# Softmax on ScalarE while weights are narrowed: the added constant and the normalization change engines

## The chip, the cores and the metric

The kernel runs on 1 core of one Trainium2 chip. The metric is the device time of one execution in microseconds (us); less is better. Engines: PE is TensorE, DVE is VectorE, ACT is ScalarE, POOL is GpSimd, SP issues DMAs.

## The reference

Three layers follow each other: a local attention, a feed-forward layer and eight experts with a balanced gate. What the change touches is the softmax of the first.

```python
scores = scale * np.matmul(q, k.transpose(0, 1, 3, 2)) + bias   # 2 batches, 8 heads, 768 tokens, 64 wide
scores = np.where(keep, scores, -1000000000.0)                  # 8 global keys, 96 local ones
a = np.exp(scores - np.max(scores, axis=-1, keepdims=True))
a = a / (np.sum(a, axis=-1, keepdims=True) + 1e-09)
attn = np.matmul(a, v)                                          # then (1536, 512)
h = x @ w_in; x = (h * (1.0 / (1.0 + np.exp(-h)))) @ w_out      # w_in (512, 2048), w_out (2048, 512)
```

Then each of 8 experts adds `P[:, e] * (max(x @ w1[e], 0) @ w2[e])`, with `P` from eight rounds of row and column normalization. `w_in` and `w_out` arrive as 64-bit floats.

## The kernel before

**Attention.** Twelve query tiles of 128 tokens, `k` = 0 to 11; each is worked in two units (`k`, `m`) of four heads. `att_turn` transposes q and k, `att_scores` does the softmax of one unit, `att_flip` transposes the weights, `att_out` multiplies by v and writes the tile `x1` as a rounded part `xh` (ACT, line 813) and a remainder `xl` (DVE, line 814). In `att_scores`, for each of two pairs of heads: PE writes the scores; DVE adds the distance table and takes the minimum (line 755); ACT takes the exponential and its sum (line 759); DVE adds 1e-9 to two sums (line 763) and inverts them (line 764); POOL multiplies each head's row by its inverse (line 767). A unit with `k` = 0 or 6 works on 128 keys, all others on 256.

**Narrowing.** Each of 16 slices of `w_in` and `w_out` is loaded as 64-bit words (`ra`, `rb`, at most 3 slices at a time, lines 129 and 132) and made a 32-bit float `wf` in `narrow`: ACT takes an absolute value `m` (line 197), DVE does four bit operations for each half (lines 203, 205, 207, 209), 8 in a slice, 128 in all. `split` rounds a slice to a high part on ACT (line 224) and takes the low part on POOL (line 225). A narrowed slice is stored to memory by a DMA on ACT's queue (line 179) for later blocks, and only then is its `wf` buffer free; there are five.

**Feed-forward layer.** Hidden steps: PE multiplies (lines 241 to 243), ACT takes a tanh (line 260), DVE makes `g` (line 261), ACT rounds it to `hh` (line 262), POOL or DVE takes the remainder `hl` (line 264), and two steps later PE multiplies by `w_out` (line 280). Steps 0 to 7 take half of the first 512 tokens each, with slices 0 to 3; from step 8 on a step takes all 512 and one slice.

**Order.** `banded` first runs tiles 0 and 1 (`startup` is true), then tiles 2 and 3 beside steps 0 to 7, then tiles 4 to 7 beside the rest of the first token block (`narrowing` is true for both), then the rest. In `go`, attention, narrowing (`pump`) and splitting (`feed`) are written between the steps at a set rate. A scheduler then places the instructions of each engine from that program; each engine works its queue in order. The constants' pool has a pad of `PAD_L` bytes that keeps the later addresses.

`copy` already chooses an engine by the same condition:

```python
        if self.startup or self.narrowing:
            self.nc.scalar.activation(dst, src, AF.Copy)
        else:
            self.nc.vector.tensor_copy(dst, src)
```

Of the kernel before, what the change touches and what calls it, by code (L numbers as in the profile page):

```python
# [8 lines left out]
F32 = mybir.dt.float32  # L9
# [5 lines left out]
AF = mybir.ActivationFunctionType  # L15
ALU = mybir.AluOpType
# [4 lines left out]
P = 128  # L21
# [7 lines left out]
EPS = 1e-9  # L29
# [7 lines left out]
RING = 4  # L37
HB = TB // 2
ORDER = 0, 5, 4, 3, 6, 1, 2
PAD_L, PAD_R = 224, 96  # L40
HALF, LINE = 64, 256
TINY = 1.125 * 2.0**-15

# [5 lines left out]
class Kernel:  # L49
# [29 lines left out]
    def setup(self, const, pre):  # L79
        nc = self.nc  # L80
        n16 = const.tile([P, 2, 4], U16, tag="n16", name="n16")
        for i, src in enumerate((self.n_global, self.n_local)):
            nc.sync.dma_start(
                n16[:, i, :], src.bitcast(U16).rearrange("(o f) -> o f", o=1).broadcast_to([P, 4])
            )
        self.att_load(0, pre)
        self.att_load(1, const)
        self.ident = const.tile([P, P], F32, tag="ident", name="ident")
        make_identity(nc, self.ident)
        rel, key = self.places(pre)  # L90
        self.ones = const.tile([P, P], F32, tag="ones", name="ones")
        nc.gpsimd.memset(self.ones, 1.0)

        ps = self.aps("warm")
        for _ in range(WARM):
            nc.tensor.matmul(ps[:, :P], self.ident, self.ident, start=True, stop=True)

        half = const.tile([P, 2, 4], F32, tag="half", name="half")
        nc.vector.tensor_copy(half, n16)
        nf = const.tile([P, 2], F32, tag="nf", name="nf")  # L100
        nc.vector.tensor_copy(nf, n16[:, :, 3].bitcast(I16))
        for i in (2, 1, 0):
            nc.vector.scalar_tensor_tensor(nf, nf, 65536.0, half[:, :, i], op0=ALU.mult, op1=ALU.add)
        self.ng, self.nl = nf[:, 0:1], nf[:, 1:2]
        fl = const.tile([P, 3], F32, tag="fl", name="fl")
        nc.vector.tensor_scalar(fl[:, 0:1], self.nl, 1.0, None, op0=ALU.is_ge)
        nc.vector.scalar_tensor_tensor(fl[:, 1:2], self.nl, float(L + 1), fl[:, 0:1], op0=ALU.is_le, op1=ALU.mult)
        flag = const.tile([P, 1], I32, tag="flag", name="flag")
        nc.vector.scalar_tensor_tensor(flag, self.ng, float(G), fl[:, 1:2], op0=ALU.is_le, op1=ALU.mult)
        self.flag = flag  # L110

        const.tile([P, PAD_L // 4], F32, tag="pad", name="pad")
        for _ in self.att_turn(0, const):
            pass
        self.tables(const, pre, rel, key)
# [613 lines left out]
    def att_scores(self, k, m):  # L729


        nc, pool = self.nc, self.ap
        a = self.att[k]
        qT, kT = a["qT"], a["kT"]
        n = W if k % self.QT else P
        a["s", m] = s = pool.tile([P, 4, W], F32, tag="s", name=f"s_{k}_{m}", bufs=LAG + 1)
        st = pool.tile([P, 3, 4], F32, tag="st", name=f"st_{k}_{m}", bufs=LAG + 2)
        banks = [self.aps(f"s_{k}_{m}_{j}") for j in range(2)]
        dst = [bank[:, x * W:x * W + n] for x in range(2) for bank in banks]
        ops = ((0, 0), (0, 1), (1, 0))[:3 if len(qT) > 1 else 1]  # L740
        for x in range(2):
            c = 2 * m + x
            for i, (y, z) in enumerate(ops):
                for j in range(2):
                    jj = slice(j * self.D, (j + 1) * self.D)
                    nc.tensor.matmul(
                        dst[2 * x + j], qT[y][jj, c * P:(c + 1) * P], kT[z][jj, c, W - n:],
                        start=i == 0, stop=i == len(ops) - 1,
                    )
        for x in range(2):  # L750
            for h in (2 * x, 2 * x + 1):
                th = self.tab[4 * m + h]
                sx = s[:, h, W - n:]

                nc.vector.tensor_tensor_reduce(  # L755
                    out=sx, in0=dst[h], in1=th[:, :W] if n == W else th[:, W:], scale=1.0, scalar=BIGMIN,
                    op0=ALU.add, op1=ALU.min, accum_out=st[:, 0, h:h + 1],
                )
                nc.scalar.activation(
                    sx, sx, AF.Exp, bias=st[:, 0, h:h + 1], scale=-1.0, accum_out=st[:, 1, h:h + 1]  # L760
                )
            two = slice(2 * x, 2 * x + 2)
            nc.vector.tensor_scalar(st[:, 2, two], st[:, 1, two], EPS, None, op0=ALU.add)  # L763
            nc.vector.reciprocal(st[:, 2, two], st[:, 2, two])  # L764
            for h in (2 * x, 2 * x + 1):
                sx = s[:, h, W - n:]
                nc.gpsimd.tensor_scalar(sx, sx, st[:, 2, h:h + 1], 1.0, op0=ALU.mult, op1=ALU.mult)  # L767
            yield

    def att_flip(self, k, m):  # L770
# [425 lines left out]
```

## Time and profile before

| what | value |
|---|---|
| median of 3 runs | 1407.94 us (1407.59 to 1408.5) |
| the profiled execution | 1407.18 us, its span 1405.3 us |
| PE busy in the span | 1375.1 us (98%), 8552 matmuls |
| DVE busy | 728.6 us (52%) |
| ACT busy | 487.8 us (35%) |
| POOL busy | 555.0 us (39%) |

The span runs from the first to the last instruction. The shares are means over parts of the program with different limits, so the first 160 us, which hold the change, are to be read by themselves.

### The profile page before, as it was taken

The numbers are of one execution on the slowest core, as the hardware profiler recorded it, in microseconds if no ns is written. First come the engines' busy times: TensorE is split into PE (matmuls) and PEld (weight loads), VectorE is DVE, ScalarE is ACT, GpSimd is POOL, SyncE is SP. The second block draws the span as 40 slices with busy tenths as digits, with TensorE's granted clock in tenths as the row PEclk, the third lists the DMA queues.
The fourth block names the chain that finished last, engine by engine and source line by source line (L and its number), as shares of the span: only waits on it lengthen the run. The fifth ranks groups of instructions, "written<-read, shape, count | busy, mean of one in ns | idle before, by whom it ended". The sixth has DMA issues, their size and how long they took to land.

```text
span 1405.3 us, 21277 instructions
## 1 busy us (share of the span) xinstructions
PE 1375.1 (98%) x8552; PEld 1205.5 (86%) x8552; DVE 728.6 (52%) x1298; ACT 487.8 (35%) x949; POOL 555.0 (39%) x489
## 2 busy tenths in 40 slices
PE   7889899999999999999999999999999999999998
PEld 5767687878889989989998998999899899989987
DVE  8999445546236466444444444444444444444443
ACT  5765555555344322223222222322222232222220
POOL 5688656534454331414333141433314143331210
PEclk8999999999999999999999999999999999999999
DMA  9785432222230101001020111102010110200001
GB/s 262 202 250 189 147 108 89 90 76 90 75 105 2 60 15 46 31 31 30 31 61 16 45 31 31 31 31 60 16 46 31 30 31 31 61 16 31 1 32 63
DMA packets 75293, 92.19 MB, mean 66 GB/s; under 512 B 30640, under 2 KB 49072, under 8 KB 75184
## 3 DMA queue, kind: packets, MB, share of 16 engines
q1 hardware_dynamic: 72880, 82.34, 19.3%
q10 hardware_dynamic: 2304, 8.39, 1.6%
q8 instruction: 69, 1.13, 0.3%
q14 instruction: 40, 0.33, 0.1%
HBM read 79.19 MB, written 11.53 MB: 65 GB/s over the span
## 4 chain that ended last, share of the span: by engine, by line
PE 89%; DVE 9%; issue 1%; ACT 1%; DMA 0%; POOL 0%; ACTq 0%; DVEq 0%; SPq 0%
PE y L442 37%; PE h L407 33%; PE y L280 7%; PE h L241 3%; PE h L242 2%; PE h L243 2%; DVE wf L205 2%; PE a_o L805 1%; DVE wf L203 1%; DVE wf L207 1%; DVE wf L209 1%; DVE s L755 1%; PE a_f L782 1%; DVE st L763 1%; DVE g L261 0%
## 5 line engine op out<-in xcount | busy, mean ns | idle before, releaser
L442 PE MATMUL y<-wx1h,room_hh 128*128 128x512 f32 x464 | 181.0, 390 | 0.0
L442 PE MATMUL y<-wx1l,room_hh 128*128 128x512 f32 x464 | 180.8, 390 | 0.0
L442 PE MATMUL y<-wx1h,room_hl 128*128 128x512 f32 x464 | 180.5, 389 | 0.0
L407 PE MATMUL h<-xc,wx0h 128*128 128x256 f32 x1024 | 176.5, 277 | 0.0
L460 DVE SCALAR_TENSOR_TENSOR x<-y,gate,x 128x512 f32<-128x512 f32 x168 | 117.4, 751 | 99.6 <-PE y L442 99.6
L362 POOL TENSOR_TENSOR wx1l<-wf,wx1h 128x512 fp32r<-128x512 f32 x64 | 82.8, 1294 | 206.5 <-ACT wx1h L361 206.5
L407 PEld LDWEIGHTS h<-xc,wx0h 128*128 128x128 f32 x1024 | 154.5, 188 | 0.1
L362 POOL TENSOR_TENSOR wc0l<-wf,wc0h 128x512 fp32r<-128x512 f32 x16 | 21.2, 1322 | 314.1 <-ACT wc0h L361 314.1
L407 PE MATMUL h<-xc,wx0l 128*128 128x256 f32 x512 | 141.6, 277 | 0.0
L421 ACT ACTIVATE room_hh<-tabs 128x512 fp32r<-128x512 f32 x87 | 54.8, 631 | 221.7 <-DVE tabs L429 200.5
L429 DVE TENSOR_TENSOR tabs<-tabs,h 128x512 f32<-128x512 f32 x144 | 95.0, 685 | 37.0 <-PE h L407 35.4
L493 DVE TENSOR_TENSOR tabs<-tabs,h 128x512 f32<-128x512 f32 x48 | 33.0, 688 | 150.3 <-PE h L407 150.3
L442 PE MATMUL y<-wx1h,room_g 128*128 128x512 f32 x304 | 106.0, 389 | 0.0
L442 PEld LDWEIGHTS y<-wx1h,room_hl 128*128 128x128 f32 x464 | 87.1, 188 | 18.4
L442 PEld LDWEIGHTS y<-wx1h,room_hh 128*128 128x128 f32 x464 | 87.1, 188 | 17.3
L442 PEld LDWEIGHTS y<-wx1l,room_hh 128*128 128x128 f32 x464 | 87.1, 188 | 16.9
L407 PEld LDWEIGHTS h<-xc,wx0l 128*128 128x128 f32 x512 | 96.1, 188 | 0.0
L422 DVE SCALAR_TENSOR_TENSOR room_hl<-tabs,room_hh 128x512 fp32r<-128x512 f32 x87 | 70.5, 811 | 41.5 <-ACT room_hh L421 40.0
L225 POOL TENSOR_TENSOR w0l<-wf,w0h 128x512 fp32r<-128x512 f32 x48 | 66.8, 1392 | 42.1 <-ACT w0h L224 41.5
L280 PE MATMUL y<-hh,w1h 128*128 128x512 f32 (+1 forms) x208 | 82.3, 396 | 0.0
L225 POOL TENSOR_TENSOR w1l<-wf,w1h 128x512 fp32r<-128x512 f32 x48 | 65.0, 1354 | 43.0 <-ACT w1h L224 39.1
L767 POOL TENSOR_SCALAR s<-s,st 128x256 f32<-128x256 f32 (+1 forms) x96 | 67.1, 711 | 36.0 <-DVE st L764 12.1
(239 smaller groups left out, 3392.6 us busy)
## 6 DMA issues: line engine op xcount, KB each, us to landing
wf<-in_moe_w_dram SPq DMA_DIRECT2D x64, 512.0 KB, 3.6
wf<-w SPq DMA_DIRECT2D x32, 512.0 KB, 3.2
ra<-in_moe_w_in_dram SPq DMA_DIRECT2D x16, 512.0 KB, 6.5
rb<-in_moe_w_out_dram SPq DMA_DIRECT2D x16, 512.0 KB, 5.1
w<-wf ACTq DMA_DIRECT2D x16, 512.0 KB, 3.8
vw<-in_v_dram SPq DMA_DIRECT2D x8, 448.0 KB, 4.7
qr<-in_q_dram SPq DMA_DIRECT2D x12, 256.0 KB, 5.0
kr<-in_k_dram SPq DMA_DIRECT2D x12, 256.0 KB, 5.6
```

Of the source, the lines that this page charges most:

```text
L225: nc.gpsimd.tensor_tensor(lo, src, f32(hi), op=ALU.subtract)
L241: nc.tensor.matmul(ps, ah, bh, start=i == 0, stop=False)
L280: nc.tensor.matmul(self.y[i][:, cols], a, b, start=begin and j == 0, stop=f == self.NF1 - 1 and j == 2, skip_group_check=True,)
L362: self.nc.gpsimd.tensor_tensor(dst[1], src, f32(dst[0]), op=ALU.subtract)
L407: nc.tensor.matmul(ps[:, f * HB:(f + 1) * HB], a[:, k, fs], b[:, k, :], start=first and n == 0, stop=n == 11, skip_group_check=True,)
L421: self.nc.scalar.activation(hi, src, AF.Relu)
L422: self.mark = self.nc.vector.scalar_tensor_tensor(lo, src, 0.0, f32(hi), op0=ALU.max, op1=ALU.subtract)
L429: self.nc.vector.tensor_tensor(c, a, b, op=op)
L442: nc.tensor.matmul(self.y[i], a, b, start=k == 0 and j == 0, stop=k == 3 and j == 2, skip_group_check=True)
L460: nc.vector.scalar_tensor_tensor(acc, self.y[i], self.gate[:, t, e:e + 1], acc, op0=ALU.mult, op1=ALU.add)
L493: nc.vector.tensor_tensor(u3, s1, b2, op=ALU.add)
L767: nc.gpsimd.tensor_scalar(sx, sx, st[:, 2, h:h + 1], 1.0, op0=ALU.mult, op1=ALU.mult)
```

## The change

A constant tile `eps` is set once. While `startup` or `narrowing` holds (tiles 0 to 7), the addition of 1e-9 is an ACT instruction with `eps` as its bias, and the normalization is an ACT copy with the inverse as its scale. The reciprocal stays on DVE. Tiles 8 to 11 are as before. The pad shrinks by 32 bytes for the new tile.

```diff
-PAD_L, PAD_R = 224, 96
+PAD_L, PAD_R = 192, 96
...
+        self.eps = const.tile([P, 1], F32, tag="eps", name="eps")
+        nc.gpsimd.memset(self.eps, EPS)
...
             two = slice(2 * x, 2 * x + 2)
-            nc.vector.tensor_scalar(st[:, 2, two], st[:, 1, two], EPS, None, op0=ALU.add)
+            busy = self.startup or self.narrowing
+            if busy:
+                nc.scalar.activation(st[:, 2, two], st[:, 1, two], AF.Identity, bias=self.eps)
+            else:
+                nc.vector.tensor_scalar(st[:, 2, two], st[:, 1, two], EPS, None, op0=ALU.add)
             nc.vector.reciprocal(st[:, 2, two], st[:, 2, two])
             for h in (2 * x, 2 * x + 1):
                 sx = s[:, h, W - n:]
-                nc.gpsimd.tensor_scalar(sx, sx, st[:, 2, h:h + 1], 1.0, op0=ALU.mult, op1=ALU.mult)
+                if busy:
+                    nc.scalar.activation(sx, sx, AF.Copy, scale=st[:, 2, h:h + 1])
+                else:
+                    nc.gpsimd.tensor_scalar(sx, sx, st[:, 2, h:h + 1], 1.0, op0=ALU.mult, op1=ALU.mult)
```

Line numbers of the changed kernel are 2 higher from the constants on and 9 higher after the softmax; its addition on ACT is line 767, its reciprocal 770, its normalization 774.

The scheduler moves other instructions too. On ACT, at the softmax of tile 2 beside hidden step 1 (`s` scores, `st` their sums, `g` and `hh` of the hidden step), there stood before:

```order
L759 ACTIVATE s_2_0_585,st_2_0_586<-s_2_0_585,st_2_0_586 128x256 x4
L260 ACTIVATE g_1_615<-h_1_549 128x256
L759 ACTIVATE s_2_1_625,st_2_1_626<-s_2_1_625,st_2_1_626 128x256 x2
L262 ACTIVATE hh_1_613<-g_1_615 128x256
L759 ACTIVATE s_2_1_625,st_2_1_626<-s_2_1_625,st_2_1_626 128x256 x2
```

In the changed kernel the same place reads:

```order
L761 ACTIVATE s_2_0_587,st_2_0_588<-s_2_0_587,st_2_0_588 128x256 x3
L767 ACTIVATE st_2_0_588<-st_2_0_588,eps_140 128x2
L761 ACTIVATE s_2_0_587,st_2_0_588<-s_2_0_587,st_2_0_588 128x256
L774 ACTIVATE s_2_0_587<-s_2_0_587,st_2_0_588 128x256 x2
L767 ACTIVATE st_2_0_588<-st_2_0_588,eps_140 128x2
L262 ACTIVATE g_1_617<-h_1_551 128x256
L761 ACTIVATE s_2_1_627,st_2_1_628<-s_2_1_627,st_2_1_628 128x256
L774 ACTIVATE s_2_0_587<-s_2_0_587,st_2_0_588 128x256 x2
L264 ACTIVATE hh_1_615<-g_1_617 128x256
```

Between an addition and its two normalizations stand one or two other instructions, and the hidden step's `g` and `hh` stand behind softmax instructions that were not there.

On DVE, between the remainders `xl` of tiles 2 and 3 (`a_o_2` and `a_o_3`), the narrowing of slices 5 and 6 stood before:

```order
L814 TENSOR_TENSOR x1_0xl_242<-a_o_2_802,x1_0xh_240 128x4x128
L205 SCALAR_TENSOR_TENSOR wf_5_961<-rb_5_569,wf_5_961 128x512
L203 TENSOR_SCALAR wf_6_1050<-ra_6_711 128x512
L207 SCALAR_TENSOR_TENSOR wf_5_961<-rb_5_569,wf_5_961 128x512
L205 SCALAR_TENSOR_TENSOR wf_6_1050<-ra_6_711,wf_6_1050 128x512
L209 SCALAR_TENSOR_TENSOR wf_5_961<-m_5_1_964,wf_5_961 128x512
L207 SCALAR_TENSOR_TENSOR wf_6_1050<-ra_6_711,wf_6_1050 128x512
L203 TENSOR_SCALAR wf_6_1050<-rb_6_712 128x512
L205 SCALAR_TENSOR_TENSOR wf_6_1050<-rb_6_712,wf_6_1050 128x512
L814 TENSOR_TENSOR x1_0xl_242<-a_o_3_856,x1_0xh_240 128x4x128
```

In the changed kernel the same place reads:

```order
L823 TENSOR_TENSOR x1_0xl_244<-a_o_2_804,x1_0xh_242 128x4x128
L211 SCALAR_TENSOR_TENSOR wf_4_884<-m_4_0_885,wf_4_884 128x512
L211 SCALAR_TENSOR_TENSOR wf_4_884<-m_4_1_887,wf_4_884 128x512
L823 TENSOR_TENSOR x1_0xl_244<-a_o_3_858,x1_0xh_242 128x4x128
L205 TENSOR_SCALAR wf_5_963<-ra_5_570 128x512
L205 TENSOR_SCALAR wf_5_963<-rb_5_571 128x512
L207 SCALAR_TENSOR_TENSOR wf_5_963<-ra_5_570,wf_5_963 128x512
L207 SCALAR_TENSOR_TENSOR wf_5_963<-rb_5_571,wf_5_963 128x512
L263 SCALAR_TENSOR_TENSOR g_4_917<-g_4_917,h_4_880 128x256
```

There only slice 4 is being finished; slices 5 and 6 begin after tile 3. On ACT's queue the stores of slices 0 to 3 and the absolute values of slices 5 and 6 likewise come after tile 3.

## Rows read from the trace of the kernel before

**Rows 1.** Windows of stages A, B, C and the next: busy time and count.

```profile
core 0: us, PE busy (x) PEld busy (x) DVE busy (x) ACT busy (x) POOL busy (x), PEclk, DMA share, GB/s
7.80:40.40 32.60, 26.11 (x163) 17.66 (x161) 31.56 (x90) 24.02 (x63) 22.01 (x28) 0.79 0.96 276
40.40:75.20 34.80, 32.06 (x256) 27.09 (x256) 33.99 (x97) 26.09 (x74) 22.55 (x30) 1.00 0.78 221
75.20:154.10 78.90, 66.22 (x372) 51.93 (x371) 74.51 (x152) 46.78 (x115) 67.25 (x58) 0.90 0.63 203
154.10:202.40 48.30, 48.30 (x271) 38.72 (x270) 13.65 (x31) 24.78 (x49) 30.52 (x30) 0.99 0.47 139
```

**Rows 2.** Chain of waits of stages A, B, C: shares by line.

```profile
by line: DVE wf L203 13.0%; PE a_o L805 9.7%; issue 9.6%; POOL s L767 8.5%; DVE s L755 8.0%; PE a_f L782 6.7%; DVE wf L209 6.6%; DVE wf L205 5.9%; DVE tabs L645 5.7%; DVE wf L207 4.0%; PE a_qr L715 3.1%; ACT s L759 2.8%; DVE x_0xl L814 2.2%
...
by line: DVE wf L207 15.6%; DVE wf L205 13.8%; DVE s L755 13.1%; issue 11.8%; DVE wf L209 10.8%; DVE wf L203 10.4%; ACT s L759 5.6%; DVE st L763 5.3%; DVE g L261 4.7%; DVE x_0xl L814 3.5%; ACT hh L262 2.3%; DVE st L764 2.1%; ACTq L179 0.9%;
...
by line: DVE wf L205 18.3%; DVE wf L207 11.7%; DVE wf L203 11.4%; DVE wf L209 11.1%; issue 8.1%; DVE st L763 5.8%; DVE s L755 5.5%; DVE g L261 4.3%; PE a_o L805 4.1%; PE h L241 3.4%; PE y L280 3.3%; PE h L243 2.5%; PE h L242 2.3%; ACT s L75
```

**Rows 3.** What PE waited for from 7.8 to 154.1 us (in all, times, longest).

```profile
PE h L241 <- DVE g L261: 11.2, 8, 3.2
PE a_f L782 <- POOL s L767: 4.6, 4, 2.0
```

**Rows 4.** Durations by line: minimum/median/maximum in ns, first and last start, forms.

```profile
L763 DVE TENSOR_SCALAR st<-st x48: 143/170/1253, 12.4 to 275.8; 128x2 f32<-128x2 f32 x48
...
L759 ACT ACTIVATE s<-s,st x96: 384/496/514, 11.5 to 275.2; 128x256 f32<-128x256 f32 x80, 128x128 f32<-128x128 f32 x16
...
L767 POOL TENSOR_SCALAR s<-s,st x96: 369/483/4467, 13.1 to 277.8; 128x256 f32<-128x256 f32 x80, 128x128 f32<-128x128 f32 x16
```

**Rows 5.** The timeline at 86 us: POOL's subtraction and DVE's addition (start, length, engine).

```profile
85.86 1.30 POOL L225 TENSOR_TENSOR w0l<-wf,w0h 128x512 fp32r<-128x512 f32 x1
...
86.12 1.07 DVE L763 TENSOR_SCALAR st<-st 128x2 f32<-128x2 f32 x1
```

**Rows 6.** The windows again, with line 763 alone.

```profile
7.80:40.40 32.60, 1.64 (x8) 0.79 0.96 276
40.40:75.20 34.80, 2.60 (x9) 1.00 0.78 221
75.20:154.10 78.90, 5.86 (x12) 0.90 0.63 203
```

**Rows 7.** Line 205 on DVE: its group (busy, mean ns), and its durations.

```profile
L205 DVE SCALAR_TENSOR_TENSOR wf<-rb,wf 128x512 uint32<-128x512 uint32 x16 | 15.2, 948 | 0.1
L205 DVE SCALAR_TENSOR_TENSOR wf<-ra,wf 128x512 uint32<-128x512 uint32 x16 | 13.8, 862 | 0.1
...
L205 DVE SCALAR_TENSOR_TENSOR wf<-rb,wf x16: 666/694/1792, 17.1 to 146.0; 128x512 uint32<-128x512 uint32 x16
```

**Rows 8.** The windows again, with line 767 alone.

```profile
7.80:40.40 32.60, 10.63 (x16) 0.79 0.96 276
40.40:75.20 34.80, 11.34 (x17) 1.00 0.78 221
75.20:154.10 78.90, 25.07 (x26) 0.90 0.63 203
```

**Rows 9.** The timeline from 83 to 86 us, ACT alone.

```profile
83.38 0.67 ACT L197 ACTIVATE m<-ra 128x512 f32<-128x512 f32 x1
84.68 0.51 ACT L759 ACTIVATE s<-s,st 128x256 f32<-128x256 f32 x1 [0.64 <-DVE st L755]
85.09 0.19 ACT L759 ACTIVATION_READ_ACCUMULATOR s<-s,st 128x1 f32 x1
```

**Rows 10.** The chain of waits from 60 to 70 us: start, length, what.

```profile
63.05 0.60 DVE wf L207
63.65 0.60 DVE wf L205
```

**Rows 11.** The page's DMA issues: stores of narrowed slices (KB, us to landing).

```profile
w<-wf ACTq DMA_DIRECT2D x16, 512.0 KB, 3.8
```

## The prediction

> **What bounds the kernel now.** I read the windows by stage first [rows 1], then the chain of waits of the same stages [rows 2], then what TensorE (PE) waited for [rows 3]. In [rows 1] see where each engine is full. From 154.1 us on PE is busy without a gap (48.30 of 48.30 us), and from there it bounds the kernel. Before that it does not. I cut that part at the ends of three `g` multiplications (line 261, hidden steps 0, 5 and 14): stage A is 7.8 to 40.4 us, B 40.4 to 75.2, C 75.2 to 154.1. In A VectorE (DVE) is busy 31.56 of 32.60 us, in B 33.99 of 34.80, in C 74.51 of 78.90; PE stands below that in each, and its granted clock is 0.79 in A and 0.90 in C. The chain [rows 2] says the same: the four narrowing lines 203 to 209 lead it in B and C, the softmax's addition (line 763) takes 5.3% and 5.8% of it, and in A the normalization on GpSimd (POOL, line 767 of the kernel before) takes 8.5%. PE's own waits [rows 3] end on the `g` that stands in DVE's queue, 11.2 us in 8 waits, and on POOL's normalization, 4.6 us in 4. So until 154 us every microsecond taken off DVE's queue counts, as long as nothing else fills up; after it nothing counts. From hidden step 15 on, which begins about there, the instruction order is the same in both kernels on all engines.
>
> **The change, part by part.** Units 0 to 7 of the query tiles are touched, that is 32 of 48 additions and 64 of 96 normalizations.
>
> *The additions leave DVE.* One on two numbers per partition takes 143 ns at its shortest and 1253 ns at its longest [rows 4]. The long ones are waits: the one at 86.12 us took 1.07 us and ended at 87.19, just after POOL's `w0l` subtraction (85.86 and 1.30 long, so to 87.16) [rows 5]. DVE loses by that 1.64 us in A, 2.60 in B, 5.86 in C [rows 6].
>
> *The normalizations leave POOL.* They lengthen DVE's other instructions in the same way. Line 205 takes 905 ns in the mean (948 and 862) where its shortest is 666 [rows 7], 0.24 us too much; over 128 narrowing instructions that is 31 us, an estimate. How much of it is line 767's no view separates. The lower bound is 0. The upper bound is its share of POOL's busy time in the three stages, 47.0 of 111.8 us [rows 1, 8], so 42% or 13 us. I take 4.8 us, near the lower: an instruction is met in proportion to its length and leaves half of it to wait, so the square of the length counts; 59 of 0.48 us [rows 4] weigh 14, the other 57, 1.14 us in the mean [rows 1, 8], weigh 74, and 14 of 88 of 31 us is 4.9. By line 767's time in the stages that is 1.1 us in A, 1.2 in B, 2.6 in C.
>
> *ScalarE (ACT) gets both.* The nearest row is the exponential of the same shape with the same kind of column operand: 496 ns for 256 numbers, 384 for 128 [rows 4]. An instruction starts some 0.10 us before the one ahead has ended (84.68 and 0.51 long, the next at 85.09) [rows 9], so a normalization occupies 0.40 or 0.28 us. For the addition no row fits: from the slope of those two it lasts 0.27 us and occupies 0.17; bounds are 0.09 (the accumulator read's 0.19 less the overlap) and 0.28. ACT gets 6.8 us in A (8 of 0.40, 8 of 0.28, 8 additions) and 7.8 in B.
>
> The Trainium skill, "ScalarE: Activation LUTs", section "Rules for kernel authors", speaks against this: for adding and multiplying it says to use VectorE, not ScalarE. By that rule the move loses. The trace agrees as to the free instruction (0.143 us on DVE against 0.17 on ACT); it disagrees as to the placed one, since the 29 additions up to 154 us took DVE 10.1 us, or 0.35 each [rows 6].
>
> *The order moves.* The scheduler places the program anew. I counted narrowing instructions up to the same three `g`: 28, 31 and 69 before, 34, 15 and 77 now, and 2 later. The 16 leave B because ACT is full there in the new order: the absolute values of slices 5 and 6 and the stores of slices 0 to 3 on ACT's queue come behind the softmax. A moved instruction I price at 0.60 us, its pace on the chain when free [rows 10]; the collisions stay with POOL's remaining instructions, whose number does not change. The upper bound is the 0.905 above. Slice 5 now waits on DVE for the store of slice 0, which lands some 3.8 us after its issue [rows 11]; behind that stand `g` of step 4 and slice 5 itself. In B DVE has over 10 us to spare for it, so I cost it at 0, at most 3.1 us (3.8 less the 0.68 of the `x` subtraction ahead).
>
> *The addition now comes back.* ACT waits for DVE's reciprocal before it normalizes, and everything on its queue waits with it. Before, POOL took that wait. In nearly every pair the new order puts an exponential, a copy or an absolute value between (0.4 to 0.6 us, [rows 9]); so I take 0.1 us of wait for each, 0 and 0.905 (a whole narrowing instruction) as bounds.
>
> **The sum.** A stays bound by DVE: 32.6 − 1.64 − 1.1 + 6 × 0.60 = 33.5, which is +0.9. ACT reaches 24.0 + 6.8 + 8 × 0.1 = 31.6 and hides. B becomes bound by ACT: 26.1 + 7.8 − 2.3 (four absolute values of 0.67 less 0.10, [rows 9], that move out) + 0.8 = 32.4, which is −2.4; DVE's 34.0 − 9.6 − 2.6 − 1.2 = 20.6 hides below. C is bound by DVE: −5.86 − 2.6 + 8 × 0.60 = −3.7; ACT is at 46.8 of 78.9 there, so what it gets is covered. The two late ones fall where DVE is busy 13.65 of 48.30 us and cost nothing. Together −5.2 us. The profiled execution took 1407.2 us, 1.9 more than its span of 1405.3; 1407.2 − 5.2 = 1402.0. It lies 0.8 us under the median of the runs, so I forecast **1402.5 us**.
>
> **Rivals.** *1, POOL's collisions cost the upper bound.* Then A gains 1.8 and C 4.3 us more: 1407.2 − 11.3 = 1395.9. For it: POOL is busy 67.25 of 78.90 us in C. Against it: line 767's instructions are the short ones.
>
> *2, the deferred narrowing eats the gain.* The moved instructions cost 0.905 each (+4.2 us) and the wait for the store is not hidden (+3.1): 1407.2 − 5.2 + 7.3 = 1409.3, and with one of the two about 1406 to 1407, no change. For it: DVE stands idle in B for over 10 us and must make up the work in C, where it is full.
>
> *3, ACT becomes the bound, slower.* Place: ACT's wait for the reciprocal in A and B. With a wait of w each, A changes by 8w − 1.8 (30.8 + 8w against 32.6), B by 8w − 3.2, C by −3.7; it decides from w = 0.54 us on. With a whole narrowing instruction ahead of each reciprocal, w = 0.905, it is 16 × 0.905 − 8.7 = +5.8, so 1413.0. For it: ACT's place in B is full, and a narrowing instruction can last 1.79 us [rows 7]. Against it: the fillers. The skill's rule named above falls in with this rival.
>
> That the change does nothing is excluded: the order shows the 96 new instructions on ACT.
>
> **How the numbers follow.** Forecast 0.42 (its own range 1399.5 to 1405.5, with w between 0 and 0.2 us), rival 1 0.14, rival 2 0.22, rival 3 0.22. A measurement of this kernel can tell about 0.2%, 2.8 us, from no change: faster is under 1405.1, slower over 1410.8. Faster: 0.36 of the forecast and rival 1, 0.50. Same: the forecast's upper edge 0.06, 0.18 of rival 2, 0.03 of rival 3, 0.27. Slower: 0.04 and 0.19, 0.23. The range 1392 to 1412 leaves out the far ends of rivals 1 and 3.
>
> **What would show it.** Right: line 763's share leaves the chain; the pace from step 5's `g` to step 14's falls from 78.9 to about 75 us, and from step 0's to 5's to about 32; in B ACT is busy nearly all the time and DVE is not; normalization instructions of 0.40 to 0.50 us on ACT stand right behind reciprocals. Wrong: DVE still full in B (then rival 1's or another gain), ACT idle on `st` for over 0.5 us a time (rival 3), or DVE idle behind a store of `w` (rival 2). If PE's gapless part starts at the same time as now, nothing was gained whatever else moved.

## The result, and the profile after

The changed kernel took **1419.47 us** (median of 4 runs, 1419.09 to 1421.63), the kernel before 1407.93 (4 runs, 1407.59 to 1408.50) beside it: ratio 1.0088, interval 1.0076 to 1.0099. It is slower by 11.5 us; 1402.5 had been forecast, with 1412.0 as the top of the range. The profiled execution took 1421.63 us, its span 1419.6, which is 14.3 over the span before.

Line numbers move: the exponential is line 761 now, the addition 767 (ACT), the reciprocal 770, the normalization 774 (ACT); narrowing stands at 205 to 211, the absolute value `m` at 199, the `g` multiplication at 263. The windows of the same stages, cut at the ends of the same three `g` (they answer to [rows 1]):

```profile
core 0: us, PE busy (x) PEld busy (x) DVE busy (x) ACT busy (x) POOL busy (x), PEclk, DMA share, GB/s
7.80:42.90 35.10, 26.10 (x160) 18.01 (x159) 33.80 (x87) 30.04 (x87) 10.28 (x11) 0.71 0.91 252
42.90:82.70 39.80, 36.13 (x265) 29.07 (x263) 22.62 (x72) 32.08 (x93) 11.78 (x13) 1.00 0.61 175
82.70:170.90 88.20, 76.96 (x392) 58.39 (x392) 78.07 (x157) 59.97 (x159) 38.48 (x29) 0.90 0.56 179
170.90:217.00 46.10, 46.10 (x246) 36.49 (x245) 13.96 (x23) 27.91 (x59) 29.58 (x27) 0.96 0.56 173
```

A is 35.10 us instead of 32.60, B 39.80 instead of 34.80, C 88.20 instead of 78.90: 16.8 us in all, of which 2.5 come back after C (1419.6 − 170.9 = 1248.7 against 1405.3 − 154.1 = 1251.2). PE is again busy without a gap once C is over, so the loss lies ahead of 170.9 us.

In the three stages together DVE does less: 33.80 + 22.62 + 78.07 = 134.5 us against 140.1. But it stands idle for 163.1 − 134.5 = 28.6 us, where it stood for 6.2 before. The length of A to C is DVE's work plus DVE's idle time: −5.6 and +22.4 make the +16.8. What DVE, ACT and PE waited for in these 163 us (in all, times, longest; before, PE's own waits were [rows 3]):

```profile
DVE s L757 <- PE a_s L748: 9.4, 9, 1.9
DVE st L770 <- ACT st L767: 6.6, 5, 2.8
DVE wf L205 <- DMA w<-wf: 3.9, 2, 2.3
DVE x_0xl L823 <- ACT x_0xh L822: 2.8, 3, 1.9
DVE g L263 <- ACT g L262: 2.1, 2, 1.8
DVE wf L211 <- ACT m L199: 1.7, 2, 0.8
DVE x_1xl L823 <- ACT x_1xh L822: 1.3, 1, 1.3
```

```profile
ACT s L774 <- DVE st L770: 22.0, 14, 3.8
```

```profile
PE h L243 <- DVE g L263: 6.0, 5, 2.0
PE a_s L748 <- DVE st L757: 5.5, 4, 2.1
PE a_f L791 <- ACT s L774: 4.8, 4, 2.1
```

Before, over the same stages, DVE's waits were:

```profile
DVE x_1xl L814 <- ACT x_1xh L813: 1.8, 1, 1.8
DVE g L261 <- ACT g L260: 1.1, 2, 0.6
DVE st L763 <- ACT s L759: 0.9, 2, 0.6
DVE wf L209 <- ACT m L197: 0.9, 1, 0.9
DVE x_0xl L814 <- ACT x_0xh L813: 0.8, 1, 0.8
```

DVE now waits on every side. For ACT it waits 14.5 us in all, where it waited 5.5 before; for PE's scores 9.4 and for the store that frees a `wf` buffer 3.9, where no such wait was listed before. These three, +9.0, +9.4 and +3.9, make up nearly all of the 22.4 us of added idle time. ACT waits 22.0 us in 14 pieces for DVE's reciprocal, and everything queued on ACT waits with it. The durations of the new instructions (minimum, median, maximum in ns) are what had been estimated from [rows 4], 270 for the addition and an exponential's for the normalization:

```profile
L767 ACT ACTIVATE st<-st,eps x32: 278/282/297, 12.8 to 179.0; 128x2 f32<-128x2 f32 x32
```

```profile
L774 ACT ACTIVATE s<-s,st x64: 386/495/516, 13.3 to 181.9; 128x256 f32<-128x256 f32 x48, 128x128 f32<-128x128 f32 x16
```

So it is not the price of the new instructions that failed. One of the long waits, from the timeline (start, length, engine, then the idle time ahead of it and its releaser):

```profile
107.35 0.29 ACT L767 ACTIVATE st<-st,eps 128x2 f32<-128x2 f32 x1
...
108.15 1.29 POOL L227 TENSOR_TENSOR w1l<-wf,w1h 128x512 fp32r<-128x512 f32 x1
...
108.24 1.74 DVE L207 SCALAR_TENSOR_TENSOR wf<-rb,wf 128x512 uint32<-128x512 uint32 x1
...
109.39 1.71 POOL L227 TENSOR_TENSOR w0l<-wf,w0h 128x512 fp32r<-128x512 f32 x1
110.02 1.64 DVE L209 SCALAR_TENSOR_TENSOR wf<-rb,wf 128x512 uint32<-128x512 uint32 x1
111.58 0.68 DVE L263 SCALAR_TENSOR_TENSOR g<-g,h 128x512 f32<-128x512 f32 x1
112.17 0.15 DVE L770 RECIPROCAL st<-st 128x2 f32<-128x2 f32 x1
...
112.36 0.91 ACT L774 ACTIVATE s<-s,st 128x256 f32<-128x256 f32 x2 [3.75 <-DVE st L770]
...
113.18 0.62 ACT L264 ACTIVATE hh<-g 128x512 fp32r<-128x512 f32 x1
```

The addition was done at 107.6. The reciprocal it feeds stands on DVE's queue behind two narrowing instructions and a `g`. Each of the two begins during a POOL subtraction and ends 0.54 and 0.56 us after it (1.74 and 1.64 us long, where 0.60 was the pace of a free one in [rows 10]). ACT idles 3.75 us, and `hh`, which PE multiplies by `w_out` two steps later, comes only behind the two normalizations.

### The profile page after: what moved, and what is told of

It is laid out like the page before. It is cut to its first block, busy times and chain, and to the rows that moved or that the text cites. A ratio compares the mean times of both kernels' runs of the same rounds, so it can differ in the third digit from the quotient of the medians.

```text
span 1419.6 us, 21209 instructions
## 1 busy us (share of the span) xinstructions
PE 1387.3 (98%) x8552; PEld 1211.5 (85%) x8552; DVE 724.2 (51%) x1266; ACT 515.6 (36%) x1045; POOL 502.2 (35%) x426
## 3 DMA queue, kind: packets, MB, share of 16 engines
q1 hardware_dynamic: 72880, 82.34, 19.1%
## 4 chain that ended last, share of the span: by engine, by line
PE 91%; DVE 6%; ACT 1%; issue 1%; DMA 1%; POOL 0%; SPq 0%; DVEq 0%
PE y L444 37%; PE h L409 33%; PE y L282 8%; PE h L243 3%; PE h L244 3%; PE h L245 3%; PE a_s L748 1%; DVE wf L207 1%; DVE wf L209 1%; PE a_o L814 1%; DVE wf L211 1%; PE a_f L791 1%; DVE wf L205 1%; DVE s L757 1%; PE lg L557 0%
## 5 line engine op out<-in xcount | busy, mean ns | idle before, releaser
L364 POOL TENSOR_TENSOR wc0l<-wf,wc0h 128x512 fp32r<-128x512 f32 x16 | 21.1, 1320 | 314.2 <-ACT wc0h L363 314.2
L282 PE MATMUL y<-hl,w1h 128*128 128x512 f32 (+1 forms) x208 | 79.0, 380 | 0.4 <-POOL hl L266 0.4
```

Of the source, the lines that this page charges most:

```text
L282: nc.tensor.matmul(self.y[i][:, cols], a, b, start=begin and j == 0, stop=f == self.NF1 - 1 and j == 2, skip_group_check=True,)
L364: self.nc.gpsimd.tensor_tensor(dst[1], src, f32(dst[0]), op=ALU.subtract)
```

## The experiments

All are timed against the kernel before on the same chip (its medians there 1407.39 to 1407.84 us). The first eight let the scheduler order the program anew each time, as the change does.

**One half of the change at a time.** e1 moves only the addition, e2 only the normalization:

```diff
 # e1_add_only
-                if busy:
+                if False:
                     nc.scalar.activation(sx, sx, AF.Copy, scale=st[:, 2, h:h + 1])
 # e2_norm_only
-            if busy:
+            if False:
                 nc.scalar.activation(st[:, 2, two], st[:, 1, two], AF.Identity, bias=self.eps)
```

> The 32 additions on ACT, the normalization back on POOL, so nothing on ACT waits for DVE's reciprocal. Round-trip theory (ACT waits 22 us for the reciprocal and holds what stands behind it): that wait is gone, so at most 1409, and by the 10.1 us that the additions took on DVE perhaps 1400. Load theory (30 us more on ACT are the loss): the additions are 32 x 0.17 = 5 us of them, so about 1409. Deferral theory (slices 5 and 6 moved behind tile 3): depends on the order that the scheduler makes; DVE narrowing instructions up to step 5's g near 59 again, so at most 1410.

> The 64 normalizations on ACT, the addition back on DVE. Round-trip theory: ACT still waits for DVE, now for addition and reciprocal, and DVE has its additions again: 1418 to 1428. Load theory: 25 of the 30 us stay, about 1417. Deferral theory: 1414 to 1420.

e1 took 1410.74 us (ratio 1.0025, 1.0015 to 1.0034), e2 1416.32 (1.0065, 1.0048 to 1.0082). Neither half gains; in these orders, each made anew, the version with the normalization loses more.

**One stretch at a time, and less work without a move.** e3 has the change only in the startup phase, e4 only in the narrowing phase; e7 is the kernel before without the addition at all:

```diff
 # e3_startup, e4_narrowing
-            busy = self.startup or self.narrowing
+            busy = self.startup
+            busy = self.narrowing
 # e7_no_add
-            nc.vector.tensor_scalar(st[:, 2, two], st[:, 1, two], EPS, None, op0=ALU.add)
-            nc.vector.reciprocal(st[:, 2, two], st[:, 2, two])
+            nc.vector.reciprocal(st[:, 2, two], st[:, 1, two])
```

> The change for tiles 0 and 1 alone (startup); tiles 2 to 7 as before. Deferral theory: stage A's share alone, narrowing up to step 5's g at 55 or more, total 1408 to 1412. Load theory: a quarter of the 96 instructions and of the loss, about 1411. If stage A's 2.5 us are the only cost, 1410.

> The change for tiles 2 to 7 alone; tiles 0 and 1 as before. Deferral theory: narrowing up to step 5's g stays near 49 in place of 59, stage C near 86 to 88 us, total 1415 to 1418. Load theory: three quarters of the loss, about 1416.5. With e3 the two losses should add up to 11.5 us.

> The kernel before without the addition of 1e-9 (all 48; the sums are at least 1, where a 32-bit float keeps nothing of it), normalization on POOL. The 29 additions took DVE 10.1 us in stages A to C. If what DVE is freed of counts in full: 1398. If the order or POOL's collisions take it back: 1403 to 1408.

e3: 1409.84 us (1.0014, 1.0004 to 1.0023). e4: 1410.28 (1.0019, 1.0009 to 1.0028). Together that is some 5 us of the 11.5: the parts don't add up. e7: 1409.77 (1.0016, 1.0006 to 1.0026). A kernel that only leaves work out, on the engine that bounds the stretch, became slower. The price of the instruction left out can't explain that, and it turned the study to the order.

**Single waits.** e5 takes ACT's wait for the reciprocal away (it leaves the division out), e6 issues the stores of narrowed slices from SP's queue in place of ACT's, e8 lets slices 4 and on be narrowed, and finished ones be stored, from tile 2 on:

```diff
 # e5_no_trip
-                    nc.scalar.activation(sx, sx, AF.Copy, scale=st[:, 2, h:h + 1])
+                    nc.scalar.activation(sx, sx, AF.Copy, scale=st[:, 1, h:h + 1])
 # e6_store_sp
-            self.nc.scalar.dma_start(self.scratch[n], w)
+            self.nc.sync.dma_start(self.scratch[n], w)
 # e8_limit_after
-                self.go(0, self.ends[0], 1)
-                self.limit = self.NF1
+                self.limit = self.NF1
+                self.go(0, self.ends[0], 1)
```

> The changed kernel, but the normalization on ACT multiplies by the sum itself, which ACT made, in place of the inverse; so the division is left out, and ACT no longer waits for DVE in the softmax. The same 96 instructions run on ACT. Round-trip theory: most of the 11.5 us come back, 1402 to 1411. Load theory: nothing comes back, 1417 to 1421. Deferral theory: 1415 to 1420, unless the order changes as well.

> The changed kernel with the stores of narrowed slices issued on SP's queue in place of ACT's. Deferral theory: DVE's waits for a store (2.3 and 1.7 us) and their 13.5% of the chain of stage B go, 2 to 6 us faster than the changed kernel, 1413 to 1417. Round-trip and load theories: no change, 1418 to 1421.

> The changed kernel, but the limit of 4 narrowed slices is lifted before tiles 2 and 3 in place of behind them, so that the program itself offers slices 4 and on to stage B. Deferral theory: narrowing up to step 5's g rises from 49 to about 60, stage C falls by 6 to 9 us, total 1410 to 1414. Round-trip and load theories: 1418 to 1421.

e5: 1417.94 us (1413.21 to 1418.04; 1.0062, 1.0044 to 1.0080). e6: 1415.96 (1.0058, 1.0041 to 1.0075). e8: 1417.20 (1.0075, 1.0058 to 1.0092). The medians lie 1.5 to 3.5 us under the changed kernel's, each in an order of its own; e5's and e8's intervals overlap with the changed kernel's. So none of the three waits is the loss. e5 shows why little came back: ACT's 22.0 us of waits for the reciprocal are gone, but over A to C ACT now waits for DVE's `g` in their place, 23.4 us in 10 waits, where the changed kernel has 5.1 in 4. e8 speaks against the deferred narrowing as the whole story: its C is 79.2 us long, about as short as before (78.90), but its B became 45.1 us long.

**The order held fixed.** In the next runs every queue is written out by NoSync edges (an order of issue, no wait), in the order of one kernel, while the instructions are those of the other. Only the additions and normalizations are free to stand where the scheduler finds a place for them. In the traces PE's, DVE's and POOL's instructions do stand in the wanted order. No run pins a kernel to its own order alone; p3 and p5 below, both near the time of before, show that holding the order of before does not slow the kernel by itself.

```diff
+    def pin(self):
+        dep = mybir.DependencyInfo(mybir.DependencyClass.NoSync, mybir.DependencyReason.DATA)
...
+        for e, l in seq.items():
...
+            order = [n for a, c in QUEUES[key] for n in range(a, a + c)]
+            for x, y in zip(order, order[1:]):
+                self.tc.add_manual_dep(l[y], l[x].name, dep, reason="order")
```

`seq` holds each engine's instructions but the free ones, as written in the program; `QUEUES` holds their places in the wanted order.

> The kernel before, its addition on VectorE and its normalization on GpSimd, but every other instruction of every queue in the order that the changed kernel has (the 48 additions and 96 normalizations take whatever place the scheduler then finds for them). If the order is what costs, this is as slow as the changed kernel, 1416 to 1421 us, though it has none of ScalarE's new work. If the new work on ScalarE and the waits between ScalarE and VectorE are what cost, this stays at 1406 to 1410 us. Both causes in parts: 1411 to 1415 us.

> The changed kernel, its addition and normalization on ScalarE, but every other instruction of every queue in the order that the kernel before has (the moved instructions take whatever place the scheduler finds). If the order is what costs, 1404 to 1409 us: the stage sums of the prediction then have a chance to show. If ScalarE's new work and the waits cost by themselves, it stays at 1415 to 1421 us. This and the run before it should mirror each other.

> The kernel before without the addition of the constant (the sums are at least 1, so that adding 1e-9 changes no bit of them), all else in the order of the kernel before. The run without the addition and without this order took 1409.77 us, 1.9 more than before, though it only takes work away. If that was the order, this is at or under the kernel before, 1404 to 1408 us, and a version that beats both. If it stays near 1410 us, something other than the order costs there.

p1: **1418.94 us** (1.0081, 1.0061 to 1.0100). p2: **1418.08** (1.0074, 1.0057 to 1.0091). Neither "order" nor "work" won: each alone costs nearly the whole, 11.4 and 10.5 us. (p1 runs the old work in an order that was made for the new; its normalizations took places on POOL that PE waits 7.1 us for, 4.6 before. How much of the 11.4 is those places no run separates.) p3: **1405.95** (0.9987, 0.9977 to 0.9996; 10 runs, 1404.33 to 1406.83, against 13 of before, 1406.63 to 1408.60). Between e7 and p3 the work is the same and the order differs: 3.8 us. p3 is the one version that beats both kernels, the one before by 1.6 us, less than the 0.2% named in the prediction.

p1's DVE, with none of the new work on ACT, over the 163.5 us of its stages:

```profile
DVE s L755 <- PE a_s L746: 9.9, 5, 4.5
DVE x_0xl L816 <- ACT x_0xh L815: 4.3, 2, 3.7
DVE wf L209 <- ACT m L197: 2.5, 3, 0.9
DVE wf L203 <- DMA w<-wf: 2.4, 1, 2.4
```

The waits for PE's scores and for the store are those of the changed kernel (9.4 and 3.9), so they come with the order. The additions' wait is not there, and is the work's. The other runs agree: over A to C DVE waits 7.7 to 10.9 us for PE's scores in e1, e2, e4 to e8 and s1, 2.2 in e3, and at most 0.8 in p2 to p6 and p8, which hold the order of before (4.1 in f1, which moves five of the score multiplications). The wait is a mark of a new order, not its price: e1 has 8.9 us of it, e7 7.7, and they lose 2.9 and 2.3 us.

**What in the new order?** In it PE spends longer on the same 136 score multiplications. The rows are PE's groups up to step 22's `g`, of the kernel before, of the changed kernel, of s1 below:

```profile
L746 PE MATMUL a_s<-kT,qT 64*128 64x256 f32 (+1 forms) x136 | 22.1, 393 | 0.0
```

```profile
L748 PE MATMUL a_s<-kT,qT 64*128 64x256 f32 (+1 forms) x136 | 30.4, 398 | 6.3 <-DVE st L757 5.5 <-ACT kT L679 0.4 <-DVE kT L709 0.4
```

```profile
L748 PE MATMUL a_s<-kT,qT 64*128 64x256 f32 (+1 forms) x136 | 24.5, 415 | 2.4 <-DVE kT L709 0.8 <-ACT at L795 0.8 <-DVE st L757 0.6
```

Two heads share a pair, on 64 rows each, and 5 of the 80 pairs stood apart on PE's queue before, 19 after. s1 is the changed kernel in its own order with the 19 put together again; DVE's order is left to the scheduler. The kernel holds the finished list of PE's queue; this made it from the changed kernel's (`q` the queue, `pos` an instruction's place in it):

```diff
+for a, b in zip(scores[::2], scores[1::2]):
+    if abs(pos[a] - pos[b]) > 1:
+        q.remove(a)
+        q.insert(q.index(b), a)
+QUEUES["PE"] = runs(q)
```

> The changed kernel with its own order on TensorE, ScalarE, GpSimd and SyncE, except that the 19 score multiplications whose partner (the other head of the pair, on the other 64 rows) stands 2 to 23 places further on TensorE's queue are moved to stand right before it; VectorE's order is left to the scheduler. In the changed kernel's profile TensorE is 8.3 us longer on the scores than before (30.4 against 22.1 us for 136 multiplications). If lost pairs are the main cost of the new order, that comes back in good part: 1411 to 1415 us, and the scores' busy time near 23 us. If the scores' time is only a sign of something else, 1416 to 1421 us.

s1: 1417.12 us (1414.38 to 1418.17; 1.0064, 1.0048 to 1.0079). The scores' time fell by 5.9 us, to 24.5 (near 23 had been expected), the kernel's by 2.4. Over A to C PE is busy 133.13 us in place of 139.18, but the stretch is only 1.4 us shorter, so most of PE's saved time became idle time; DVE waits 9.3 us for scores as it did. So lost pairs are mostly a symptom.

**Which work, with the order kept?**

> The order of before on every queue; the normalization on ScalarE, the addition left on VectorE. The same order with both moved took 1418.08 us, VectorE waiting 17.4 us for the addition on ScalarE. If that wait is the cost in that order, this is at 1405 to 1410 us. If the cost is the normalization's place on ScalarE (its wait for the reciprocal, and TensorE's 4.3 us of waits for it), this stays at 1413 to 1419 us.

> The order of before on every queue; the addition on ScalarE, the normalization left on GpSimd. If VectorE's wait for the addition is the cost in that order, 1413 to 1419 us; if it is the normalization, 1407 to 1411 us.

> The kernel before without the addition of the constant, in the order of before (that run took 1405.95 us), and in addition the 5 score multiplications that stand apart from their partner in it moved to stand right before it. If an unpaired one costs about 0.27 us of TensorE (four unpaired took 1.06 us where eight in pairs took 1.06 us), 1404 to 1405.5 us; if pairing is nothing, 1406 us.

(The edits are those of e2, e1 and e7, in the order of before; f1 moves the 5 pairs as s1 does.) p5: **1407.09 us** (1.0003, 0.9994 to 1.0012): the addition alone costs nothing once the order is kept, though DVE waits 5.5 us for it. That wait (17.4 us in p2) was my guess for p2's loss, and it was wrong. p4: **1421.06** (1416.04 to 1422.14; 1.0101, 1.0085 to 1.0116): the normalization does it by itself. Its profiled execution is the 1416.04 one, so what follows from its trace explains a loss of 8.7 us, not all of the 13.7 of the median. f1: 1408.82 (1.0005, 0.9996 to 1.0014), not the 1404 to 1405.5 expected: pairs put together cut the scores again, from 21.0 us in p3 to 20.2, and the kernel took 2.9 us longer than p3.

What DVE waited for in p4, over its stages:

```profile
DVE wf L211 <- ACT m L199: 7.1, 5, 2.6
DVE st L769 <- ACT s L761: 5.5, 8, 1.6
DVE g L263 <- ACT g L262: 5.5, 5, 1.5
```

The longest of these, on the timeline:

```profile
80.67 0.90 ACT L775 ACTIVATE s<-s,st 128x256 f32<-128x256 f32 x2
...
81.01 0.17 DVE L771 RECIPROCAL st<-st 128x2 f32<-128x2 f32 x1
81.47 0.89 ACT L775 ACTIVATE s<-s,st 128x256 f32<-128x256 f32 x2
82.27 0.61 ACT L226 ACTIVATE w0h<-wf 128x512 fp32r<-128x512 f32 x1
82.79 0.40 ACT L264 ACTIVATE hh<-g 128x256 fp32r<-128x256 f32 x1
83.10 0.66 ACT L199 ACTIVATE m<-ra 128x512 f32<-128x512 f32 x1
83.79 1.02 DVE L211 SCALAR_TENSOR_TENSOR wf<-m,wf 128x512 f32<-128x512 f32 x1 [2.62 <-ACT m L199]
```

ACT does not wait here at all. It works off four normalizations (0.90 and 0.89 us for two each), and behind them, after a split's `w0h` and `hh`, stands `m`, the one thing that DVE needs next. DVE idles 2.62 us.

**The wait, or the work?** p6 is p4 with e5's edit: no wait for the reciprocal, and no division. p8 is p4 with each normalization at least three of ACT's other instructions further back:

```diff
 # p8_norm_later_3
+            if key == "Activation":
+                for i, n in zip(self.norms, AFTER):
+                    self.tc.add_manual_dep(i, l[order[n]].name, dep, reason="order")
```

> The order of before, only the normalization on ScalarE, and scaled by the raw sum instead of its inverse, so that nothing on ScalarE waits for VectorE's reciprocal (this leaves the division of the softmax out). With the wait the same kernel took 1421.06 us. If the wait for the reciprocal, with what queues behind it on ScalarE, is the cost: 1406 to 1410 us. If it is the 64 instructions' own time on ScalarE that delays what stands behind them: 1414 to 1421 us.

> The order of before, only the normalization on ScalarE, each one put at least 3 of ScalarE's other instructions further back than the scheduler had put it, so that the reciprocal is ready when its turn comes. If only the wait costs and the flips on TensorE can take the delay: 1406 to 1411 us. If TensorE then waits for the normalization instead, or if ScalarE's time is the cost: 1414 us or more.

p6: 1414.67 us (1413.45 to 1414.73; 1.0049, 1.0032 to 1.0066). p8: **1411.24** (10 runs, 1406.91 to 1411.87; 1.0020, 1.0010 to 1.0029). Without the wait 6.9 us of p4's 13.7 remain; with the same work behind other work 3.5 remain, and the row of p4 above is down in p8 to:

```profile
DVE wf L211 <- ACT m L199: 1.6, 3, 1.0
```

So the place on ACT's queue counts: the same 64 instructions cost 10.2 us less further back. p8 does not tell place from wait, since it also takes ACT's waits for the reciprocal from 11.2 us to 4.3; p6, with none of them, puts the wait at about half of p4's loss. Over A to C DVE's waits for `m`, the exponential and `g` together are 18.1 us in p4, 12.7 in p6, 9.3 in p8 and 2.9 before. What p8 still loses lies in the rest of these and in PE, which meets some normalizations late (7.1 us, where PE waited 4.6 for POOL's before); in which, no run shows:

```profile
PE a_f L794 <- ACT s L775: 7.1, 4, 2.8
```

All runs on one measure: the length of A to C (from 7.8 us to the end of step 14's `g`) and what DVE was busy in it, from the windows of the profiled execution; idle is their difference. The time is the median, for p4 5.0 us over its profiled execution.

| kernel | time us | A to C | DVE busy | DVE idle |
|---|---|---|---|---|
| before | 1407.93 | 146.30 | 140.06 | 6.2 |
| changed | 1419.47 | 163.10 | 134.50 | 28.6 |
| e1 addition only | 1410.74 | 151.00 | 132.95 | 18.1 |
| e2 normalization only | 1416.32 | 158.20 | 134.92 | 23.3 |
| e3 startup only | 1409.84 | 149.00 | 137.46 | 11.5 |
| e4 narrowing only | 1410.28 | 153.00 | 133.95 | 19.1 |
| e5 no wait for the reciprocal | 1417.94 | 159.20 | 133.53 | 25.7 |
| e6 stores from SP | 1415.96 | 155.50 | 135.06 | 20.4 |
| e7 no addition | 1409.77 | 150.40 | 137.06 | 13.3 |
| e8 earlier narrowing | 1417.20 | 158.40 | 131.56 | 26.8 |
| p1 before, order of changed | 1418.94 | 163.50 | 141.08 | 22.4 |
| s1 changed, pairs together | 1417.12 | 161.70 | 130.83 | 30.9 |
| p2 changed, order of before | 1418.08 | 158.10 | 132.55 | 25.6 |
| p4 normalization, order of before | 1421.06 | 156.70 | 135.61 | 21.1 |
| p5 addition, order of before | 1407.09 | 147.40 | 139.42 | 8.0 |
| p6 p4 without the wait | 1414.67 | 154.00 | 135.88 | 18.1 |
| p8 p4, normalization later | 1411.24 | 150.70 | 136.13 | 14.6 |
| p3 no addition, order of before | 1405.95 | 144.90 | 138.83 | 6.1 |
| f1 p3, pairs together | 1408.82 | 148.30 | 139.63 | 8.7 |

Every version but p1 took busy time off DVE, 0.4 to 9.2 us of it. None but p3 took time off the kernel, 1.6 us (p5's 0.3 lie within its interval). DVE's idle time tells fast from slow, roughly; its busy time does not. Every version that idles under 15 us is at most 3.5 us slower than before, every one over 20 us at least 8.1; e1, e4 and p6, at 18 to 19 us, lose 2.9, 2.8 and 6.9.

## Why the prediction was wrong

- **What bounds the kernel: right as a reading, wrong as a rule.** DVE was full in A to C, and PE without a gap behind it. But "every microsecond taken off DVE's queue counts, as long as nothing else fills up" is the step that failed. Nothing else filled up: in C ACT is busy 59.97 of 88.20 us, in B 32.08 of 39.80, and DVE still idled, 28.6 us in place of 6.2. The condition should have read: as long as nothing that DVE waits for comes later.
- **C, −3.7 forecast, +9.3 measured: the largest miss.** It has two parts. DVE's idle time in C grew by 5.7 us (10.1 in place of 4.4). And DVE's busy time, forecast to fall by 3.7, rose by 3.6: the sums `st` fell by 5.4, near the 5.86 forecast, but the narrowing rose by 6.9, where −2.6 and +8 × 0.60 had made it +2.2. These are DVE's narrowing instructions in C, before and after:

```profile
75.20:154.10 78.90, 56.90 (x69) 0.90 0.63 203
```

```profile
82.70:170.90 88.20, 63.83 (x77) 0.90 0.56 179
```

  At 0.82 and 0.83 us each they took as long as before, so the moved ones cost nearer rival 2's 0.905 than 0.60, and no gain from POOL shows in C. As to the idle time, "ACT is at 46.8 of 78.9 there, so what it gets is covered" took a mean share for cover. p4 shows, with the order kept, what normalizations on ACT can do: DVE waits 18.1 us for `m`, the exponential and `g`, and p8 that their place matters. In the changed kernel's own C, though, DVE waits 3.4 us for ACT (`g` and a remainder), 4.8 for PE's scores and 1.7 for a store: less of it is ACT's than in p4, and the waits for scores and store come with the new order.

- **B, −2.4 forecast, +5.0 measured.** ACT reached 32.08 us there, almost the 32.4 of the sum, but B was not bound by ACT: it is 39.80 long, and its chain is led by PE and the store (the lines of the chain of waits that answer to [rows 2]):

```profile
by line: PE y L282 15.5%; PE a_s L748 14.3%; DMA w<-wf 13.6%; PE a_f L791 7.9%; DVE wf L209 7.8%; DVE s L757 6.4%; DVE wf L207 5.7%; DVE wf L205 5.5%; PE a_o L814 4.0%; PE h L243 3.9%; PE h L245 2.4%; PE h L244 2.4%; DVE wf L211 2.2%; ACT s
```

  With 15 narrowing instructions in place of 31 DVE has nothing to do while it waits for scores. The wait for slice 0's store was costed "at 0, at most 3.1 us"; waits for a store are 2.3 us there and 3.9 in all.
- **A, +0.9 forecast, +2.5 measured.** Bound by DVE as said: it is busy 33.80 of 35.10 us, where a length of 33.5 had been forecast.
- **The additions leave DVE: over-priced.** The 10.1 us of 29 additions were counted as saved in full. p3 takes them out and leaves the order. The rows are DVE's busy time on the sums `st` and on the narrowing's `wf`, over A to C, of the kernel before and of p3:

```profile
7.80:154.10 146.30, 18.37 (x118) 0.90 0.74 224
...
7.80:154.10 146.30, 100.80 (x128) 0.90 0.74 224
```

```profile
7.80:152.70 144.90, 8.67 (x89) 0.93 0.74 226
...
7.80:152.70 144.90, 106.67 (x128) 0.93 0.74 226
```

  `st` fell by 9.7 us, the same 128 narrowing instructions took 5.9 longer. That fits a DVE that is held while POOL subtracts [rows 5]: take the held addition out, and the next instruction is held in its place. The two groups together lose 3.8 us, about the additions' shortest time, 29 × 0.143 = 4.1 us [rows 4]; all of DVE's instructions together lose only 1.2 (140.06 to 138.83), and A to C is 1.4 us shorter.
- **The normalizations leave POOL: right in total, not by stage.** 4.8 us had been taken off the narrowing: 1.1 in A, 1.2 in B, 2.6 in C. In p4, which keeps the order, `wf` is 96.64 us, 4.2 less, far from rival 1's 13; but it is 2.7 less in A, 2.9 less in B and 1.5 more in C, so the agreement of the total is in part luck. It did not help, since DVE then waited. In the changed kernel it does not show at all (100.22 us for 126 instructions, 100.80 for 128 before).
- **The wait for the reciprocal: w was mis-sized.** 0.1 us for each was taken, on the ground that "in nearly every pair the new order puts an exponential, a copy or an absolute value between". It is 22.0 us in 14 waits over the 32 pairs, 0.69 each, and above the 0.54 from which rival 3 decides. But rival 3 had put it in A and B, where it is 1.3 and 1.1; 19.6 fall in C. And its removal in e5 gave back 1.5 us, since ACT then waited for `g`. The bound of a single wait, one narrowing instruction, was too low too: two and a `g` stood ahead in the 3.75 us above. Rival 3's 1413.0 was on the right side, and its mechanism is a part only.
- **Rival 2, deferred narrowing.** B shows its idle DVE and its wait for the store. That the count of deferred instructions alone sets the loss, e8 and p2 exclude: e8 has 70 done by the end of B in place of 49, p2 has the order of before on DVE, and they took 1417.20 and 1418.08 us.
- **The scheduler's order.** It was counted for 16 instructions only. p1 shows that the new order costs 11.4 us with the old work in it, and e7 against p3 that a new order costs 3.8 where work is only left out. The order is also not the same from step 15 on, as the prediction has it, but only from 182.8 us (before) and 197.0 us (now); nothing hung on that, since PE is full there in both.
- **The Trainium skill's rule** that was named against the change (the Trainium skill, "ScalarE: Activation LUTs", "Rules for kernel authors": adding and multiplying belong on VectorE) pointed to the right side. For the addition alone, with the order kept, the runs don't bear it out (p5, 1407.09 us). The normalization came from GpSimd, and no run puts it on VectorE, so the rule is not tested there; what its move cost depended on its place on ScalarE's queue (p4, p8).

**What stays open.** Order and work each cost about 11 us alone and 11.5 together. Why they don't add was not found; it may be that once DVE idles 20 us and more, other engines' queues set the length. Which feature of the new order costs is open too: pairs (2.4 us in s1), deferral and the store were tried one by one, and none was the whole; DVE's wait for scores comes with every new order but e3's, and why the scores come late there was not followed up.

## What to carry to other kernels

An engine that is busy 60% of a stretch (ACT in C, before) is no cover by that alone: on an in-order queue, what counts is whether the added instruction stands ahead of something that the full engine waits for. So list, for each added instruction, what is behind it on its queue and who waits for that. A long duration on an engine that shares something may be a wait; here removing the instruction handed most of the wait to others, so price it at no more than its shortest time. And where a scheduler orders the program, a small edit is also a new order: before judging the edit, run it once in the old order and the old work once in the new.

## What the runs showed of the hardware

Score multiplications of two heads, on 64 rows each, share PE's time when they stand next to each other on its queue. Eight in pairs take as long as four of which none has its partner beside it (PE's timeline of the kernel before, then of the changed one: start, length, count):

```profile
51.07 1.13 PE L746 MATMUL a_s<-kT,qT 64*128 64x256 f32 x8
```

```profile
106.38 1.13 PE L748 MATMUL a_s<-kT,qT 64*128 64x256 f32 x4
```

The granted clock is 1.00, the higher of its two levels, over both. That had not been looked for ahead of the change. Of the 8.3 us by which the scores are longer in the changed kernel (30.4 against 22.1), s1 gives 5.9 back by putting pairs together, and shows that most of these were not on the path. The second surprise is the one told above: 9.7 us taken off DVE came back by 5.9 as longer narrowing.
